# A two-layer GELU block on one core: the first loads dealt out over three queues

## The chip, the cores and the metric

The kernel runs on one core of one Trainium2 chip. The metric is the device time of one execution in microseconds (us); lower is better. Of the kernel before there are seven runs without a profile, and one profiled execution from which all rows and durations below are taken.

## The reference

The input x has 2048 rows (tokens) of 448 features, all tensors are bfloat16, and two dense layers with a GELU between them are applied to each row:

```python
def _gelu(x):
    return jax.nn.gelu(x, approximate=True)

B, S, D, F = 1, 2048, 448, 1792

def reference(x, w1, b1, w2, b2):
    h = jnp.einsum("bsd,df->bsf", x, w1) + b1
    h = _gelu(h)
    return jnp.einsum("bsf,fd->bsd", h, w2) + b2
```

## The kernel before

**Staging.** The 2048 rows are handled in four chunks of 512 (`c` from 0 to 3). For each chunk layer 1 computes, for 14 blocks of 128 hidden features (`ft`), the transposed hidden tile `g[:, ft, chunk]`, with ScalarE applying bias and GELU from PSUM; layer 2 then uses those tiles as stationary operands and makes four tiles of 128 rows by 448 outputs, to which VectorE adds b2 before SyncE stores them. Everything is written out by hand as one list of operations per engine; a small helper (`Program`) gives each engine its list in the order in which the operations were recorded and puts semaphore waits ahead of those that need them. The order of a queue is therefore the order of the calls in the source.

**Contraction of 448.** It is cut into three slabs of 128 (`w1_sb`, `k` = 0, 1, 2) and a rest of 64 (`w1r`). Every matmul uses 64 rows of the array, and two of them, one on each half of the rows, run side by side (a "pair"). The rest of 64 lies in partitions 64 to 127 of `w1r` and is copied by VectorE to partitions 0 to 63 for half of the feature blocks (line 380, event `w1rU`).

**Loads.** All weights come over SyncE's queue, in this order: the first x chunk, the first piece of w1 (feature blocks 0 to 3, 384 KB, called w1(0) below), the first piece of its rest (blocks 0 to 3, 64 KB, w1r(0)), w1(1) (blocks 4 to 7, 384 KB), w1r(1) (blocks 4 to 13, 160 KB), w1(2) (blocks 8 to 13, 576 KB), w2 in two parts, b2, and then the other three x chunks, which the DMA transposes on the way. ScalarE's queue carries one load, the 3.5 KB of b1 as 14 rows, and it waits for VectorE to clear the tile `b1n`. Behind it on ScalarE is a one-column GELU into `junk` (line 175), which brings in the activation table.

**The first chunk.** It isn't transposed by the DMA. It lands in `xn` as 128 partitions by four row tiles `t`, each partition holding four consecutive rows of x. TensorE transposes each tile in three steps of 128 columns (`turn`, line 337, 12 transposes) into PSUM, VectorE (t = 0, 2) and ScalarE (t = 1, 3) copy the result into `xT` (line 344). The last 64 columns of the four tiles are first gathered by VectorE into `xr` (line 351), transposed two tiles at a time (line 358) and copied out four times (line 367). TensorE needs the identity matrix for this, made by GpSimd.

**Around it.** Ahead of the transposes TensorE multiplies ones with ones into an unused PSUM bank (`warm`, line 190): seven matmuls of 512 columns and one of 256. VectorE, when it is through with the copies of the first chunk, turns b1 into one column per feature block (`turn_b1`, four 32x32-block transposes on line 179 and a cast on line 181), and then makes the two `w1rU` copies.

**Layer 1 of the first chunk.** `Layer1.a` is the three slabs of a pair of feature blocks, `Layer1.b` the same on the other half of the rows plus the rest of 64, after which ScalarE takes the two tiles. The order is `L[0].a` and `L[1].a` on the first 256 rows, the same on the second 256, `L[0].b`, `L[2].a`, `L[1].b`, `L[3].a`, `L[2].b`, and so on. `L[0]` and `L[1]` need w1(0) and w1r(0), `L[2]` and `L[3]` need w1(1) and w1r(1), `L[4]` to `L[6]` need w1(2). All these matmuls are recorded by one helper, `mm`, and so stand on line 215, as those of layer 2 do.

Of the kernel before, what the change touches and what calls it, by code (L numbers as in the profile page):

```python
# [73 lines left out]
def bass_standalone__dense_activation_gelu__prompt_kernel(  # L74
# [8 lines left out]
    B, S, D = x.shape  # L83
    F = w1.shape[1]
    P = 128
    H = P // 2
    SC = 512
    HC = SC // 2
    assert B == 1 and S % SC == 0 and F == 14 * P and D == 3 * P + H
    x2, out2 = x[0], out[0]  # L90
    NSC, NST, STC, NFT = S // SC, S // P, SC // P, F // P
    NPAIR = NFT // 2
    KT = 3
    D3 = KT * P
    DH = D // 2
    NWARM = 7

    with ExitStack() as es:
        sb = lambda name, shape, dt: es.enter_context(nc.sbuf_tensor(name, shape, dt))
        xn = sb("xn", [P, STC, D], BF16)  # L100
        xr = sb("xr", [P, STC // 2, P], BF16)
        ident = sb("ident", [P, P], BF16)
# [5 lines left out]
        b1n = sb("b1n", [32, P], BF16)  # L108
# [8 lines left out]
        pr = Program(nc, es)  # L117
# [7 lines left out]
        def w1_of(ft):  # L125
            return max(i for i, c in enumerate(W1CUTS) if c <= ft)

        def load_w1(i):
            c0, c1 = W1CUTS[i] * P, W1CUTS[i + 1] * P
            pr.dma("sync", lambda e: e.dma_start(  # L130
                w1_sb[:, :, c0:c1], w1[0:D3, c0:c1].rearrange("(k p) f -> p k f", p=P)), ("w1", i))

        RCUTS = (0, 4, 14)
# [1 line left out]
        def load_w1r(i):  # L135
            cs = slice(RCUTS[i] * P, RCUTS[i + 1] * P)
            pr.dma("sync", lambda e: e.dma_start(w1r[H:P, cs], w1[D3:D, cs]), ("w1r", i))
# [12 lines left out]

        x0v = x2[0:SC, :].rearrange("(p t) d -> p t d", t=STC)
        o0v = out2[0:SC, :].rearrange("(p t) d -> p t d", t=STC)
        pr.dma("sync", lambda e: e.dma_start(xn[:, :, :], x0v), "x")  # L153
        load_w1(0)
        load_w1r(0)
        load_w1(1)
        load_w1r(1)
        load_w1(2)
        load_w2(0, 7)
        load_w2(7, 14)  # L160
        pr.dma("sync", lambda e: e.dma_start(b2_bc[:, :], b2.partition_broadcast(P)), "b2")
        for c in range(1, NSC):
            for slot in range(KT + 1):
# [6 lines left out]
            base=0, pattern=[[-1, P]], channel_multiplier=1), after=["ident0"], event="ident")  # L170
        pr.op("gpsimd", lambda e: e.memset(b2_z[:, :], 0.0), event="b2z0")
        pr.op("vector", lambda e: e.memset(b1n[:, :], 0.0), event="b1z")  # L172
        pr.dma("scalar", lambda e: e.dma_start(b1n[0:NFT, :], b1.rearrange("(c p) -> c p", p=P)), "b1n",
               after=["b1z"])
        pr.op("scalar", lambda e: e.activation(junk[:, :], one, ACT.Gelu_apprx_tanh))  # L175

        def turn_b1():
            for q in range(4):
                pr.op("vector", lambda e, q=q: e.transpose(  # L179
                    b1t[32 * q:32 * q + 32, :], b1n[:, 32 * q:32 * q + 32]), after=["b1n"], event=("b1t", q))  # L180
            pr.op("vector", lambda e: e.tensor_copy(b1_f[:, :], b1t[:, 0:NFT]),
                  after=[("b1t", q) for q in range(4)], event="b1")
# [5 lines left out]
        def warm(n, cols=SC):  # L188
            for _ in range(n):
                pr.op("tensor", lambda e: e.matmul(unit[2][:, 1, 0:cols], lhsT=ones_w, rhs=ones_m[:, 0:cols],  # L190
                                                   start=True, stop=True))
# [140 lines left out]
        def stage(t):  # L332
            return unit[3 - t // 2][:, t % 2, 0:2 * P].bitcast(BF16)

        def turn(t):
            for k in range(KT):
                pr.op("tensor", lambda e, k=k: e.transpose(  # L337
                    stage(t)[:, k * P:(k + 1) * P], xn[:, t, k * P:(k + 1) * P], ident[:, :]),
                    after=["ident", "x"], event=("xt", t) if k == KT - 1 else None)

        def evac(engine, t):
            o = xT[:, 0:KT, t * P:(t + 1) * P]
            i = stage(t)[:, 0:D3].rearrange("p (k s) -> p k s", k=KT)
            pr.op(engine, lambda e: e.copy(o, i) if engine == "scalar" else e.tensor_copy(o, i),  # L344
                  after=[("xt", t)], event=("xT0", t))
            busy[(3 - t // 2, t % 2)] = ("xT0", t)

        def turn_all():


            pr.op("vector", lambda e: e.tensor_copy(
                xr[:, :, :].rearrange("p q (two h) -> p q two h", two=2),
                xn[:, :, D3:D].rearrange("p (q two) h -> p q two h", two=2)), after=["x"], event="xr_in")
            for t in range(STC):
                turn(t)
                evac(("vector", "scalar")[t % 2], t)
            for q in range(STC // 2):
                pr.op("tensor", lambda e, q=q: e.transpose(
                    stage(0)[:, q * P:(q + 1) * P], xr[:, q, :], ident[:, :]),
                    after=["xr_in", ("xT0", 0)], event=("xr", q))  # L360
            halves = (slice(0, H), slice(H, P))
            for src, engine in enumerate(("vector", "scalar")):
                i = stage(0)[halves[src], 0:2 * P].rearrange("p (q s) -> p q s", q=2)
                for dst in (src, 1 - src):
                    o = xT[halves[dst], KT, 0:SC].rearrange("p (q two s) -> p q two s", q=2, two=2)[:, :, src, :]
                    pr.op(engine, lambda e, o=o, i=i, engine=engine:
                          e.copy(o, i) if engine == "scalar" else e.tensor_copy(o, i),  # L367
                          after=[("xr", 0), ("xr", 1)], event=("xR0", dst, src))
            busy[(3, 0)] = ("xR0", 1, 0)
            busy[(3, 2)] = ("xR0", 0, 1)  # L370

        warm(NWARM)
        warm(1, HC)
        turn_all()
        turn_b1()

        for i in (0, 1):
# [3 lines left out]
                  after=[("w1r", i)], event=("w1rU", i))  # L381
# [12 lines left out]
        for c in range(NSC):  # L394
# [7 lines left out]
            else:  # L402

                pr.op("vector", lambda e: e.tensor_copy(b2_z[H:H + 1, :], b2_bc[H:H + 1, :]),  # L404
                      after=["b2", "b2z0"], event="b2z")
# [3 lines left out]
            p = Layer2(c, (0, 1))  # L409
            if c + 1 < NSC:  # L410
                q = Layer2(c, (2, 3))
# [5 lines left out]
            else:  # L417
                q, r = Layer2(c, (2,)), Layer2(c, (3,), True)
# [37 lines left out]
```

## Time and profile before

| what | value |
|---|---|
| median of 7 runs | 94.23 us (94.01 to 94.62) |
| the profiled execution's own time | 94.71 us |
| its span, first to last instruction | 93.4 us |
| TensorE matmul busy | 90.0 us (96%), 931 instructions |
| ScalarE busy | 38.5 us (41%) |
| VectorE busy | 13.4 us (14%) |
| first matmul of layer 1 | at 6.12 us |
| loads from HBM, written back | 3.79 MB, 1.84 MB |

The profile's page gives busy time of each engine, the chain of work that ended last and the costliest groups of instructions. Times in the views are us from the start of the span. PE is TensorE's matmuls, PEld its weight loads, DVE VectorE, ACT ScalarE, POOL GpSimd, SP SyncE; a q behind a name is the engine's queue of DMA issues. Names of tiles are shown without numbers, so that `w_sb` is either weight of the two layers and `u` any of the four PSUM units. The 1.3 us between span and time (94.71 less 93.4) lie outside of what the profile shows.

### The profile page before, as it was taken

What the parts mean: (1) busy time and instruction counts of PE and PEld (TensorE: products, weight loads), DVE (VectorE), ACT (ScalarE), POOL (GpSimd) and SP (SyncE); (2) the same over time, 40 slices, a digit from 0 to 9 for tenths busy, and PEclk for the clock granted to TensorE, in tenths of its full rate; (3) what the DMA queues carried; (4) which work ended last, traced back from release to release, by engine and by line L of the source; (5) the groups of instructions that cost most, each with busy time, mean ns of one, the idle gap of its engine ahead of it and who ended that gap; (6) DMA issues with size and microseconds to landing.
All of it is one profiled execution on the core that took longest, in us unless ns stands there. A gap on an engine that the chain in (4) does not pass through costs nothing.

```text
span 93.4 us, 2058 instructions
## 1 busy us (share of the span) xinstructions
PE 90.0 (96%) x931; PEld 46.6 (50%) x931; DVE 13.4 (14%) x33; ACT 38.5 (41%) x63; POOL 1.1 (1%) x7
## 2 busy tenths in 40 slices
PE   6989999999999999999999999999999999999990
PEld 2465444555544444455554444455554444475890
DVE  0173101010334000000234000000234000000421
ACT  3373787900002787900002888900001878910001
POOL 4000000000000000000000000000000000000000
PEclk9999999999999999999999999999999999999999
DMA  1999999754937100000032000000022000000022
GB/s 55 316 265 273 378 357 97 142 113 91 107 74 193 46 0 0 7 0 0 0 105 98 0 0 4 0 7 0 0 98 98 0 7 0 0 0 7 21 78 98
DMA packets 12340, 7.32 MB, mean 78 GB/s; under 512 B 6956, under 2 KB 12140, under 8 KB 12332
## 3 DMA queue, kind: packets, MB, share of 16 engines
q1 hardware_dynamic: 12304, 7.20, 32.6%
q8 instruction: 7, 0.11, 0.5%
q14 instruction: 1, 0.01, 0.0%
q10 hardware_dynamic: 28, 0.00, 0.0%
HBM read 3.79 MB, written 1.84 MB: 60 GB/s over the span
## 4 chain that ended last, share of the span: by engine, by line
PE 91%; DMA 5%; SPq 0%; DVE 0%; issue 0%
PE u L215 91%; DMA w_sb<-in_w_dram 5%; SPq L153 0%; DVE out_sb L324 0%
## 5 line engine op out<-in xcount | busy, mean ns | idle before, releaser
L267 ACT ACTIVATE g<-u,b_f 128x512 bf16<-128x512 f32 x56 | 35.0, 685 | 40.2 <-PE u L215 40.2
L215 PE MATMUL u<-w_sb,g 64*128 64x448 bf16 (+1 forms) x504 | 43.2, 328 | 0.0
L215 PE MATMUL u<-xT,w_sb 64*128 64x512 bf16 (+1 forms) x348 | 40.9, 369 | 0.4 <-DMA w_sb<-in_w_dram 0.4
L215 PEld LDWEIGHTS u<-w_sb,g 64*128 64x128 bf16 x504 | 24.5, 94 | 18.4
L215 PEld LDWEIGHTS u<-xT,w_sb 64*128 64x128 bf16 x348 | 16.8, 94 | 19.6 <-DMA w_sb<-in_w_dram 0.9
L310 DVE TENSOR_TENSOR out_sb<-u,b_bc 128x448 bf16<-128x448 f32 x14 | 8.1, 619 | 60.0 <-PE u L215 60.0
L215 PE MATMUL u<-xT,w1r 64*128 64x512 bf16 x56 | 10.6, 376 | 0.0
L215 PEld LDWEIGHTS u<-xT,w1r 64*128 64x128 bf16 x56 | 2.8, 94 | 3.3
L327 ACT CAST out_sb<-u 128x224 bf16<-128x224 f32 x1 | 0.3, 345 | 9.2 <-PE u L215 9.2
L190 PE MATMUL u<-const-bfloat16-1.0 128*128 128x512 bf16 (+1 forms) x8 | 3.4, 598 | 0.8 <-PEq L441 0.8
L190 PEld LDWEIGHTS u<-const-bfloat16-1.0 128*128 128x128 bf16 x8 | 1.0, 136 | 2.4 <-issue 2.4
L175 ACT ACT_TABLE_LOAD x1 | 1.3, 1283 | 1.6 <-DVE b1n L172 1.6
L344 ACT COPY xT<-u 128x384 bf16<-128x384 bf16 x2 | 1.0, 478 | 2.0 <-PE u L337 2.0
L337 PEld LDWEIGHTS u<-ident,xn 128*128 128x128 bf16 x12 | 1.2, 144 | 0.6 <-issue 0.6
L337 PE MATMUL u<-ident,xn 128*128 128x128 bf16 x12 | 1.4, 310 | 0.0
L185 DVE COPY xT<-xT 64x512 bf16<-64x512 bf16 x3 | 0.9, 290 | 3.8 <-DMA xT<-in_x_dram 3.8
L404 DVE COPY b_z<-b_bc 1x448 bf16<-1x448 bf16 x1 | 0.3, 268 | 5.4 <-DMA b_bc<-in_b_dram 5.4
L318 DVE TENSOR_TENSOR out_sb<-u,b_bc 128x448 bf16<-128x448 f32 x1 | 0.6, 624 | 1.7 <-PE u L215 1.7
L179 DVE STREAM_TRANSPOSE b1t<-b1n 32x32 bf16<-32x32 bf16 x4 | 0.8, 202 | 0.1
L344 DVE COPY xT<-u 128x384 bf16<-128x384 bf16 x2 | 0.7, 358 | 0.7 <-PE u L337 0.7
L380 DVE COPY w1r<-w1r 64x256 bf16<-64x256 bf16 (+1 forms) x2 | 0.6, 288 | 1.5 <-DMA w1r<-in_w_dram 1.4
L367 ACT COPY xT<-u 64x256 bf16<-64x256 bf16 x2 | 0.7, 368 | 0.0
(17 smaller groups left out, 4.1 us busy)
## 6 DMA issues: line engine op xcount, KB each, us to landing
out_dram<-out_sb SPq DMA_DIRECT2D x16, 112.0 KB, 1.7
w_sb<-in_w_dram SPq DMA_DIRECT2D x2, 784.0 KB, 9.5
w_sb<-in_w_dram SPq DMA_DIRECT2D x2, 384.0 KB, 5.4
w_sb<-in_w_dram SPq DMA_DIRECT2D x1, 576.0 KB, 7.3
xn<-in_x_dram SPq DMA_DIRECT2D x1, 448.0 KB, 3.2
xT<-in_x_dram SPq DMA_TRANSPOSE x12, 4.5
w1r<-in_w_dram SPq DMA_DIRECT2D x1, 160.0 KB, 6.5
b_bc<-in_b_dram SPq DMA_DIRECT2D x1, 112.0 KB, 9.6
```

Of the source, the lines that this page charges most:

```text
L175: pr.op("scalar", lambda e: e.activation(junk[:, :], one, ACT.Gelu_apprx_tanh))
L179: pr.op("vector", lambda e, q=q: e.transpose(b1t[32 * q:32 * q + 32, :], b1n[:, 32 * q:32 * q + 32]), after=["b1n"], event=("b1t", q))
L185: pr.op("vector", lambda e: e.tensor_copy(xT[0:H, KT, s0:s1], xT[H:P, KT, s0:s1]), after=after, event=event)
L190: pr.op("tensor", lambda e: e.matmul(unit[2][:, 1, 0:cols], lhsT=ones_w, rhs=ones_m[:, 0:cols], start=True, stop=True))
L215: o = pr.op("tensor", lambda e: e.matmul(unit[u][:, lo, cols], lhsT=lhsT, rhs=rhs, start=start, stop=stop, skip_group_check=skip), after=a ...
L267: pr.op("scalar", lambda e, lo=lo, ft=ft: e.activation(g[:, ft, c * SC:(c + 1) * SC], unit[u][:, lo, :], ACT.Gelu_apprx_tanh, bias=b1_f[:, ...
L310: pr.op("vector", lambda e, lo=lo, j=j: e.tensor_tensor(out=out_sb[:, j, :], in0=unit[u][:, lo, 0:D], in1=b2_bc[:, :], op=ALU.add), after= ...
L318: pr.op("vector", lambda e: e.tensor_tensor(out=out_sb[:, j, :].rearrange("p (two h) -> p two h", two=2), in0=unit[u][:, :, 0:DH], in1=b2_ ...
L337: pr.op("tensor", lambda e, k=k: e.transpose(stage(t)[:, k * P:(k + 1) * P], xn[:, t, k * P:(k + 1) * P], ident[:, :]), after=["ident", "x ...
L344: pr.op(engine, lambda e: e.copy(o, i) if engine == "scalar" else e.tensor_copy(o, i), after=[("xt", t)], event=("xT0", t))
L367: e.copy(o, i) if engine == "scalar" else e.tensor_copy(o, i),
L380: pr.op("vector", lambda e, odd=odd: e.tensor_copy(odd(slice(0, H)), odd(slice(H, P))), after=[("w1r", i)], event=("w1rU", i))
```

## The change

The first x chunk is loaded as two halves (row tiles 0 and 1, row tiles 2 and 3), one from SyncE's queue and one from ScalarE's, with a semaphore each; each row tile's transposes wait for their own half, and the gathering copy into `xr` becomes two copies. w1(1) leaves SyncE's queue and is issued from ScalarE's, recorded behind the one-column GELU. b1's load moves from ScalarE's queue to GpSimd's, behind the three operations that GpSimd does at the start. The warm-up becomes six matmuls of 512 columns.

```diff
-    NWARM = 7
+    NWARM = 6
...
-        def load_w1(i):
+        def load_w1(i, engine="sync"):
             c0, c1 = W1CUTS[i] * P, W1CUTS[i + 1] * P
-            pr.dma("sync", lambda e: e.dma_start(
+            pr.dma(engine, lambda e: e.dma_start(
...
-        pr.dma("sync", lambda e: e.dma_start(xn[:, :, :], x0v), "x")
+        for h, engine in ((0, "sync"), (2, "scalar")):
+            pr.dma(engine, lambda e, h=h: e.dma_start(xn[:, h:h + 2, :], x0v[:, h:h + 2, :]), ("x", h))
         load_w1(0)
         load_w1r(0)
-        load_w1(1)
         load_w1r(1)
         load_w1(2)
...
-        pr.dma("scalar", lambda e: e.dma_start(b1n[0:NFT, :], b1.rearrange("(c p) -> c p", p=P)), "b1n",
+        pr.dma("gpsimd", lambda e: e.dma_start(b1n[0:NFT, :], b1.rearrange("(c p) -> c p", p=P)), "b1n",
                after=["b1z"])
         pr.op("scalar", lambda e: e.activation(junk[:, :], one, ACT.Gelu_apprx_tanh))
+        load_w1(1, "scalar")
...
-                    after=["ident", "x"], event=("xt", t) if k == KT - 1 else None)
+                    after=["ident", ("x", t // 2 * 2)], event=("xt", t) if k == KT - 1 else None)
...
-            pr.op("vector", lambda e: e.tensor_copy(
-                xr[:, :, :].rearrange("p q (two h) -> p q two h", two=2),
-                xn[:, :, D3:D].rearrange("p (q two) h -> p q two h", two=2)), after=["x"], event="xr_in")
             for t in range(STC):
+                if t % 2 == 0:
+                    pr.op("vector", lambda e, t=t: e.tensor_copy(
+                        xr[:, t // 2, :].rearrange("p (two h) -> p two h", two=2), xn[:, t:t + 2, D3:D]),
+                        after=[("x", t)], event=("xr_in", t // 2))
                 turn(t)
...
-                    after=["xr_in", ("xT0", 0)], event=("xr", q))
+                    after=[("xr_in", q), ("xT0", 0)], event=("xr", q))
...
         warm(NWARM)
-        warm(1, HC)
```

## The prediction

> **What bounds the kernel now.** I read the chain of waits first, in order of time.
>
> ```profile
> 1.19 4.89 DMA w_sb<-in_w_dram
> 6.08 0.05 issue
> 6.12 85.08 PE u L215 x909
> ```
>
> From 6.12 us TensorE is the chain without a break to the end, 85.08 us long. Ahead of it stands one load: w1(0), issued at 1.19, landed at 6.08. Nothing that the change touches lies behind 16.5 us, where layer 2 begins, so its worth is how much earlier or later layer 1 of the first chunk starts, and whether it then still runs through. Next the timeline of TensorE's matmuls and the other engines over the first microseconds (start, us, engine, line, operation).
>
> ```profile
> 0.77 3.36 PE L190 MATMUL u<-const-bfloat16-1.0 128*128 128x512 bf16 x8 [0.77 <-PEq L441]
> 3.96 0.23 DVE L351 COPY xr<-xn 128x256 bf16<-128x256 bf16 x1 [3.04 <-DMA xn<-in_x_dram]
> 4.07 1.44 PE L337 MATMUL u<-ident,xn 128*128 128x128 bf16 x12
> 5.30 0.42 PE L358 MATMUL u<-ident,xr 128*128 128x128 bf16 x2
> 6.12 2.13 PE L215 MATMUL u<-xT,w_sb 64*128 64x256 bf16 x30 [0.40 <-DMA w_sb<-in_w_dram]
> 8.29 0.98 PEld L215 LDWEIGHTS u<-xT,w_sb 64*128 64x128 bf16 x12 [0.21 <-DMA w_sb<-in_w_dram]
> 0.95 0.62 ACTq L173 DMA_DIRECT2D b1n<-in_b_dram  x1
> 1.60 1.28 ACT L175 ACT_TABLE_LOAD   x1 [1.60 <-DVE b1n L172]
> ```
>
> x lands just before 3.96, the transposes are over at 5.72, TensorE waits 0.40 us, for w1(0) and not for x. The weight load at 8.29 shows a second wait: `L[2].a` needs w1(1), which arrives with nothing to spare. The source line of w1's three loads gives their times from issue to landing, and the windows how full the DMA engines are meanwhile (columns: window, its length, PE, PEld, DVE, ACT, POOL busy, granted clock, DMA share, GB/s).
>
> ```profile
> DMA to landing us min/median/max: 4.9/6.0/7.3
> ...
> 1.50:3.20 1.70, 1.70 (x5) 0.59 (x4) 0.00 (x0) 1.49 (x2) 0.37 (x1) 1.00 0.76 264
> 3.20:4.70 1.50, 1.50 (x10) 0.81 (x9) 0.34 (x2) 0.00 (x0) 0.00 (x0) 1.00 0.96 282
> 4.70:6.10 1.40, 1.03 (x10) 0.76 (x8) 0.87 (x3) 1.00 (x3) 0.00 (x0) 1.00 0.97 297
> 6.10:8.30 2.20, 2.18 (x32) 1.58 (x34) 1.51 (x8) 0.69 (x2) 0.00 (x0) 1.00 1.05 231
> 8.30:11.00 2.70, 2.70 (x28) 1.27 (x28) 0.35 (x1) 2.25 (x4) 0.00 (x0) 1.00 1.07 353
> ```
>
> With the issues at 1.19, 2.25 and 3.41 (SP's queue) the three land at 6.08, 8.25 and 10.7. The engines' share is 0.96 and more from 3.2 us on: they are full, and the order of the bytes is what decides.
>
> **x in two halves, and the warm-up.** The 448 KB of x move in the windows up to 3.2 us; TensorE sees them complete at 3.95, so some 0.7 us pass between the last bytes and the wait's end. If the first half goes first, its 224 KB are through by about 2.5 (half of 1.75 to 3.2) and it lands near 3.2. Six warm-ups at 0.43 each (weight loads of line 190 at 2.01, 2.43, 2.86) end at 0.77 + 6 x 0.43 = 3.35, so the transposes begin at about 3.4 instead of 4.07. The second half lands where x lands now, 3.95; tiles 0 and 1 take 6 x 0.107 = 0.64, to 4.05, so tiles 2 and 3 do not wait. All 14 transposes end near 5.05 instead of 5.72. That is 0.65 us less on a branch which already waits 0.40 for w1(0): worth nothing alone. The `xr` gather becomes two copies of some 0.2 us; the second waits for the second half on VectorE, with the copy of tile 2 queued behind it, which needs the same half. Cover: the same wait for w1(0).
>
> **w1(0) against w1(1).** Bytes ahead of w1(0) stay the same, x's 448 KB, for both halves are issued with it or before. New is a rival on another queue. ScalarE issues the second half at about 0.73, taking 0.4 to 0.6 (rows of SP's first issue, 0.39, and of b1, 0.62), loads its table for 1.28 and runs the GELU for 0.20, so that w1(1) is issued near 2.8; x's first data came 1.0 after its issue, hence w1(1)'s at about 3.75. By then w1(0) has had 3.75 - 3.2 = 0.55 us at 282 GB/s, 155 thousand of its 393 thousand bytes (384 KB). Shared equally, the other 238 thousand take 1.69 instead of 0.84 us: w1(0) lands **0.84 later**. If ScalarE's queue issues without waiting for the table load, the two share from 3.2 on, and 393 thousand bytes take 2.79 instead of 1.39: **1.39 later**. The other end: taking turns may be coarse. The DMA view by window has b1's packets (queue q10) as evidence: issued at 0.95, none moved before 3 us, all of them between 3.0 and 3.5, as x's last ones left.
>
> ```profile
> q1 hardware_dynamic: 101, 0.14, 80.5%
> q10 hardware_dynamic: 28, 0.00, 4.7%
> ```
>
> If w1(1) stands behind w1(0) in that way, the cost is 0. Below nothing: if two queues fill the engines better, at the 353 GB/s of the last window instead of some 275, the 852 thousand bytes of x and w1(0) take 2.41 instead of 3.10 us, but some of that lies in the slow first microsecond; I take **0.5 earlier** as that end. Within -0.5 to +1.39 I take +0.65, nearer to the case worked out from ScalarE's own rows (+0.84) than to 0, because b1's row speaks for turns that are not fine.
>
> The Trainium skill, DMA: Bandwidth & Descriptors, section "Issuing engines are not separate DMA queues", holds that DMAs of all queues run on the same 16 engines and interleave, so that a second queue saves only the issuing time. It speaks against this change; by it alone the sum would be +0.84 to +1.39, and the rows of full engines agree with its first half, while b1's row does not show an even interleaving.
>
> **w1(1) and those behind it.** It is needed 2.18 us after the start (8.30 less 6.12), at 8.95 if the start is 6.77. From 3.75 at half of 231 to 282 GB/s its 393 thousand bytes take 2.8 to 3.4, to 6.6 to 7.2, and 1.4 to 2 more pass to the landing as for w1(0): 8.0 to 9.2. Cost 0 to 0.25 (no gain is possible, since at that start it is not the last to arrive); I take 0. SP moves w1r(1) and w1(2) up past it. w1(2) is needed 5.2 after the start (`L[4].a` at 11.33 now, 12.0 then), landed at 10.7, and the bytes ahead of it are the same: 0. The issues behind (w2, b2, transposes) move up by one issue, 0.58, and are not waited for before 15 us: 0.
>
> **b1 by GpSimd.** No DMA of GpSimd is in the trace. It can be issued at 1.87 (line 171's memset, 1.40 + 0.47). The nearest row is b1 on ScalarE's queue: 2.5 us from issue to its last packet, which gives 4.4. VectorE takes it up behind its `xT` copies, now at 6.47, then perhaps 5.9. Behind it on VectorE are the cast and the `w1rU` copies; their chain of 4 x 0.20 + 0.18 + 0.22, some 1.5 us with gaps, must be over at the first rest pair, 1.97 after the start (8.09 now, 8.74 then). So b1 may land as late as 7.2, 2.8 us more than the nearest row; cost 0. Without that cover it is one for one, and the upper bound is b2's 9.6 us landing, the longest of a small load here: 11.5, which would cost 4; I hold that far from the nearest row and leave it in the tail.
>
> **The sum.** 0 + 0.65 + 0 + 0. On the profiled execution's 94.71 us (span 93.4) this is 95.36; that execution lies 0.48 above the median, and on the median it is 94.23 + 0.65 = **94.9 us**. About 0.5% (0.47 us) is what a measurement here can tell from no change.
>
> **Rivals.**
> *Two queues fill the engines (faster).* w1(0) lands at about 5.6, x's branch is done at 5.05 plus the copies, and layer 1 starts 0.5 earlier: 93.7. For it: 264 to 297 GB/s now against 353 later, and the last engines' lag of 1.4 us behind the bytes. Against it: shares of 0.96 and more, and w1(1) then has to land 0.5 earlier also, at 7.8, or `L[2].a` takes the gain back. It decides once w1(0) lands before 5.65.
> *The load is as late as before (same).* Turns are so coarse that w1(1) waits for w1(0), the start stays near 6.1, and the earlier x is waste: 94.2. b1's packets speak for it.
> *The clock comes late (slower).* Warm-ups of 512 columns stand 0.43 apart, six pairs of 512 in layer 1 take 1.30 (8.30 to 9.60), 0.22 each: the rate doubles somewhere between 5.4 and 6.12, although the granted clock reads 1.00 throughout. Now TensorE idles 0.40 before layer 1; afterwards from 5.05 to 6.77, 1.7 us. If the doubling is put off, each us of layer 1 at the old rate costs 0.5, and at most the 4.95 us (0.77 to 5.72) that it takes now: up to 2.5, and with half of it on top of 0.65 96.1. The Trainium skill, TensorE: Matmul & The Clock Gate, section "Why this matters for your kernels", asks for 4 us of continuous work and allows gaps up to about 3 us; by it this term would be nothing, and no row here shows a gap of 1.7 us.
>
> **How the numbers follow.** Main case, w1(0) later by 0.2 to 1.4: 0.44, of which 0.08 stays within 0.47 us. Faster rival 0.26. Same rival 0.17. Late clock 0.13. Faster 0.26; same 0.17 + 0.08 = 0.25; slower 0.36 + 0.13 = 0.49. The range goes from 93.6, just below the faster rival, to 96.1; the main case alone spans 94.4 to 95.6.
>
> **What would show it.** Right: transposes from about 3.4; w1(0) landing at 6.5 to 7.1 and heading the chain; queue q10 moving w1(1) between 3.5 and 7; 256-column pairs of layer 1 standing 0.11 apart. Wrong: w1(0) landed by 5.65; the weight load of `L[2].a` or VectorE's b1 transposes with a wait of over 0.3 us; 256-column pairs in layer 1 standing 0.21 apart instead of 0.11.

## The result, and the profile after

The changed kernel takes 96.04 us at the median of 12 runs (94.99 to 98.85), against 94.52 (94.00 to 94.77) of the kernel before in 31: slower by 1.31% (ratio 1.0131, 95% interval 1.0106 to 1.0157). The profiled execution takes 96.14 us and spans 94.8. The ratio leaves out executions that lie over 1.5% above the fastest of the same kernel; since one cause found below costs about that much, the medians here are over all runs.

The sign and the range of the forecast (94.9 us, 93.6 to 96.1) hold, the range by 0.06 us: 96.04 lies outside the main case's 94.4 to 95.6, and the medians are 1.52 us apart where 0.65 was forecast. The way there is another one. The chain of waits of the kernel after, in order of time (start, us, what):

```profile
1.20 4.45 DMA w_sb<-in_w_dram
5.65 0.05 issue
5.70 86.96 PE u L216 x909
```

w1(0) landed at 5.65, 0.43 us *earlier* than in the profile before, and layer 1 started 0.42 earlier. But the same 909 matmuls on line 216 (215 before) now last 86.96 us instead of 85.08. The timeline of the first microseconds shows where (start, us, engine, line, operation; the last bracket is the idle time before it and its releaser):

```profile
0.78 2.72 PE L191 MATMUL u<-const-bfloat16-1.0 128*128 128x512 bf16 x6 [0.78 <-PEq L442]
1.18 1.28 ACT L175 ACT_TABLE_LOAD   x1 [1.18 <-PEq L442]
1.24 0.44 ACTq L130 DMA_DIRECT2D w_sb<-in_w_dram  x1
3.94 1.44 PE L338 MATMUL u<-ident,xn 128*128 128x128 bf16 x12 [0.43 <-DMA xn<-in_x_dram]
5.70 4.02 PE L216 MATMUL u<-xT,w_sb 64*128 64x256 bf16 x30
7.15 0.90 DVE L180 STREAM_TRANSPOSE b1t<-b1n 32x32 bf16<-32x32 bf16 x4 [0.86 <-DMA b1n<-in_b_dram]
9.09 0.15 PEld L216 LDWEIGHTS u<-xT,w1r 64*128 64x128 bf16 x2 [0.27 <-DVE w1r L381]
9.51 0.42 PE L216 MATMUL u<-xT,w1r 64*128 64x512 bf16 x2
9.77 1.46 PE L216 MATMUL u<-xT,w_sb 64*128 64x512 bf16 x12
```

Before, the first rest pair of layer 1 stood at 8.09, 1.97 after the start at 6.12:

```profile
8.09 0.38 PE L215 MATMUL u<-xT,w1r 64*128 64x512 bf16 x2
```

The first 30 matmuls take 4.02 us instead of 2.13, and the first rest pair comes 3.81 after the start instead of 1.97: 1.84 us later, for TensorE is still at its first, half rate. Twelve pairs of 256 columns at 0.213 and three of 512 at 0.427 make 3.84. The next row, 12 matmuls in 1.46, is again as before. So 1.84 less the earlier start of 0.42 is 1.42, and the spans differ by 1.4: this execution loses all of it to TensorE's rate doubling at about 9.5 us instead of before 6.12. Ahead of it is a pause: the warm-up ends at 3.50, the transposes begin at 3.94. The wait for b1 (0.86 on VectorE, then 0.27 for a weight load) is hidden: VectorE finished both `w1rU` copies (0.49 us from 8.39 on) while TensorE was still at half rate.

The third row also corrects the order of ScalarE's queue: w1(1) was issued at 1.24, beside the table load and not behind it. Two windows (columns as in the prediction) show the engines fuller than before, 374 GB/s against 282 and 327 against 297:

```profile
3.20:4.70 1.50, 1.07 (x9) 0.80 (x9) 0.45 (x2) 0.00 (x0) 0.00 (x0) 1.00 1.06 374
4.70:6.10 1.40, 1.29 (x14) 0.90 (x13) 0.94 (x5) 1.15 (x3) 0.00 (x0) 1.00 1.13 327
```

The second queue isn't shown to be the reason. The kernel before with only b1's load moved (below), whose x and weights all come over SyncE's queue, moved 352 GB/s in the first of these windows and started layer 1 at 5.67:

```profile
3.20:4.70 1.50, 1.50 (x10) 0.79 (x9) 0.32 (x2) 0.00 (x0) 0.00 (x0) 1.00 1.07 352
```

### The profile page after: what moved, and what is told of

The parts are those of the page before. It is cut to its first block, busy times and chain, and to the rows that moved or that the text cites. A ratio compares the mean times of both kernels' runs of the same rounds, so it can differ in the third digit from the quotient of the medians.

```text
span 94.8 us, 2056 instructions
## 1 busy us (share of the span) xinstructions
PE 91.3 (96%) x929; PEld 46.8 (49%) x929; DVE 13.4 (14%) x34; ACT 38.5 (41%) x63; POOL 1.7 (2%) x8
## 3 DMA queue, kind: packets, MB, share of 16 engines
HBM read 3.79 MB, written 1.84 MB: 59 GB/s over the span
## 4 chain that ended last, share of the span: by engine, by line
PE 92%; DMA 5%; SPq 0%; DVE 0%; issue 0%
PE u L216 92%; DMA w_sb<-in_w_dram 5%; SPq L154 0%; DVE out_sb L325 0%
## 5 line engine op out<-in xcount | busy, mean ns | idle before, releaser
L216 PE MATMUL u<-xT,w_sb 64*128 64x512 bf16 (+1 forms) x348 | 42.7, 383 | 0.1
L216 PEld LDWEIGHTS u<-xT,w_sb 64*128 64x128 bf16 x348 | 17.5, 98 | 20.3 <-issue 0.5
L191 PE MATMUL u<-const-bfloat16-1.0 128*128 128x512 bf16 x6 | 2.7, 626 | 0.8 <-PEq L442 0.8
```

The source lines that it names most:

```text
L216: o = pr.op("tensor", lambda e: e.matmul(unit[u][:, lo, cols], lhsT=lhsT, rhs=rhs, start=start, stop=stop, skip_group_check=skip), after=a ...
```

## The experiments

Theories: **A**, the clock (the shorter warm-up leaves a pause, and the rate doubles late); **B**, b1 by GpSimd lands late; **C**, w1(1) on ScalarE's queue costs, by delaying w1(0) as the prediction had it or otherwise; later **D**, the parts work on one another, and **E**, C's loss comes from what SyncE sends meanwhile.

| kernel | median of all runs (range) | ratio to before (95%) |
|---|---|---|
| changed | 96.04 (94.99 to 98.85) | 1.0131 (1.0106 to 1.0157) |
| changed, old warm-up | 95.49 (94.96 to 96.74) | 1.0093 (1.0055 to 1.0132) |
| changed, b1 from ScalarE's queue | 95.99 (94.67 to 97.19) | 1.0101 (1.0059 to 1.0144) |
| both: only the loads of x and w1(1) changed | 94.88 (94.51 to 95.42) | 1.0045 (1.0024 to 1.0067) |
| before, short warm-up | 94.44 (93.93 to 96.44) | 0.9978 (0.9956 to 0.9999) |
| before, w1(1) on ScalarE's queue | 95.30 (94.42 to 96.59) | 1.0059 (1.0021 to 1.0097) |
| before, b1 by GpSimd | 94.46 (94.05 to 95.01) | 1.0012 (0.9991 to 1.0033) |
| before, x in halves | 94.41 (93.97 to 94.82) | 0.9993 (0.9968 to 1.0018) |
| before, w1(1) on ScalarE's queue and short warm-up | 95.81 (95.03 to 98.12) | 1.0136 (1.0092 to 1.0181) |
| only the loads, w1(1) after x's first half | 99.08 (97.40 to 99.95) | 1.0337 (1.0305 to 1.0370) |
| only the loads, SyncE held | 94.51 (94.02 to 94.78) | 1.0003 (0.9986 to 1.0020) |
| changed, SyncE held | 94.90 (94.68 to 98.36) | 1.0034 (1.0013 to 1.0055) |
| only the loads, SyncE held, short warm-up | 94.44 (94.05 to 96.22) | 1.0005 (0.9981 to 1.0029) |

Of 128 runs of the kernel before, taken beside these, one lies above 95.2 us, at 96.67.

**The changed kernel with the old warm-up.**

```diff
-    NWARM = 6
+    NWARM = 7
...
         warm(NWARM)
+        warm(1, HC)
```

> The changed kernel with the old warm-up (seven matmuls of 512 columns and one of 256). Theory A, the clock: the changed kernel loses because TensorE pauses 0.43 us between its shorter warm-up and the first transposes, so that the rate doubles only at about 9.5 us and layer 1's first 1.84 us are paid twice. Here the pause is gone: pairs of 256 columns stand 0.11 us apart from the first one. If A were all, layer 1 starts at 5.7 to 5.9 and the time is 94.0 to 94.3. Theory B, b1 by GpSimd: b1 lands only at 7.1, VectorE then makes the copy for the rest of 64 (w1rU) at 8.4 to 8.6, while TensorE at the full rate would want it at about 7.6: a stall near 1 us, which the slow clock hid before. A and B together: 94.9 to 95.2, with a wait for VectorE in front of the first rest pair. If neither holds and the loads are to blame, about 96 as in the changed kernel.

0.55 us less than the changed kernel at the median, and more than the 94.9 to 95.2 of A and B together. The runs of the two kernels overlap so far that the difference of the medians isn't clear of the spread. The profile says more: it has no pause, and the rate doubled before layer 1:

```profile
6.44 2.13 PE L216 MATMUL u<-xT,w_sb 64*128 64x256 bf16 x30 [1.38 <-DMA w_sb<-in_w_dram]
7.49 0.90 DVE L180 STREAM_TRANSPOSE b1t<-b1n 32x32 bf16<-32x32 bf16 x4 [1.72 <-DMA b1n<-in_b_dram]
9.01 0.09 PEld L216 LDWEIGHTS u<-xT,w1r 64*128 64x128 bf16 x1 [0.72 <-DVE w1r L382]
```

30 matmuls take 2.13 again, as A has it. B shows too, as a wait of 0.72 that the slow clock had hidden. And here w1(0) is what TensorE waits for, until 6.40: it came 0.7 later than in the profiled execution of the changed kernel, out of the same queues. Where w1(0) lands is not settled by the source. The 1.38 us for which TensorE stood idle there did not bring the half rate back.

**The changed kernel with b1 from ScalarE's queue.**

```diff
-        pr.dma("gpsimd", lambda e: e.dma_start(b1n[0:NFT, :], ...
+        pr.dma("scalar", lambda e: e.dma_start(b1n[0:NFT, :], ...
```

> The changed kernel with b1 loaded from ScalarE's queue again, behind the half of x and ahead of the table load; the short warm-up stays. Theory A alone or A with B: the clock still comes late, the missing copy was hidden by it, so 95.8 to 96.2, no wait of VectorE for b1, pairs of 256 columns 0.21 apart. Theory B alone: 94.5 to 95.0.

As A expects: the median is the changed kernel's within 0.05, and the profile has the late doubling.

```profile
5.68 3.81 PE L216 MATMUL u<-xT,w_sb 64*128 64x256 bf16 x30
```

**Both of these edits: only the loads of x and w1(1) are changed.**

> The changed kernel with the old warm-up and with b1 from ScalarE's queue: what is left of the change is x in two halves and w1(1) on ScalarE's queue. Theories A and B together: layer 1 starts at 5.7 to 5.9, runs through, 94.1 to 94.4 against 94.5 of before, since w1(0) landed 0.43 us earlier in the changed kernel. The theory of the prediction, that w1(1) on its own queue holds w1(0) up: 94.9 or more.

94.88 is slower than A and B together allow (94.1 to 94.4) and just short of what the prediction's theory asked. The start was early, at 5.32; the loss comes 3 us later (rows as above):

```profile
5.32 2.13 PE L216 MATMUL u<-xT,w_sb 64*128 64x256 bf16 x30
7.49 0.09 PEld L216 LDWEIGHTS u<-xT,w1r 64*128 64x128 bf16 x1 [0.31 <-DVE w1r L382]
8.47 1.47 PE L216 MATMUL u<-xT,w_sb 64*128 64x512 bf16 x12 [0.59 <-DMA w_sb<-in_w_dram]
```

w1(0) wins and w1(1) loses: issued at 1.94, it landed at 8.42, and `L[2].a` waits 0.59 for it. In the changed kernel itself w1(1) was in time. There b1 doesn't stand ahead of it on ScalarE's queue, it was issued at 1.24 and landed at 6.61 (at 7.24 with the old warm-up). The rows of w1(1) with KB and us from issue to landing, of the changed kernel and of this one:

```profile
w_sb<-in_w_dram ACTq DMA_DIRECT2D x1, 384.0 KB, 5.4
w_sb<-in_w_dram ACTq DMA_DIRECT2D x1, 384.0 KB, 6.5
```

So the stall of 0.59 was seen only with b1 on ScalarE's queue. The medians split the loss into 0.36 for the loads (94.52 to 94.88), 0.61 for b1 (to 95.49) and 0.55 for the warm-up (to 96.04). In the other order the warm-up costs 1.11 and b1 0.05, so some 0.56 of the loss can be put down to either of the two, and the split is no list of stalls in the changed kernel.

**The kernel before with the short warm-up alone.**

> The kernel before with the short warm-up alone (six matmuls of 512 columns). Theory A: x lands at 3.95, the warm-up ends near 3.5, a pause of 0.4 to 0.5 us as in the changed kernel, the rate doubles late; layer 1 starts at 6.1 at half rate: 95.9 to 96.6. Theory B or the loads: 94.5, the same as before.

A as stated fails here: 94.44, no slower than before. But the two slowest of its 12 runs are 95.37 and 96.44, and the one at 95.37 is the profiled one, with a pause of 0.70 and, for a part of the matmuls, the half rate (3.15 us for 30):

```profile
4.19 1.44 PE L337 MATMUL u<-ident,xn 128*128 128x128 bf16 x12 [0.70 <-DMA xn<-in_x_dram]
5.78 3.15 PE L215 MATMUL u<-xT,w_sb 64*128 64x256 bf16 x30
```

So, if the pause is the reason, it makes the late doubling possible and not certain.

**The parts, one by one, on the kernel before.** w1(1) alone on ScalarE's queue, b1 alone by GpSimd, x alone in halves, and w1(1) together with the short warm-up:

> The kernel before with w1(1) alone moved to ScalarE's queue, behind b1 and the one-column GELU; x in one piece, old warm-up. In the runs so far ScalarE's queue issued w1(1) right after the load ahead of it, without waiting for the table load. Theory C, the loads: w1(1) then moves beside x and w1(0) from about 2.6 us on, x or w1(0) lands 0.3 to 0.8 later or w1(1) itself is what TensorE waits for: 94.9 to 95.4. If two queues only fill the engines better: 94.0 to 94.4.

> The kernel before with b1's load alone moved to GpSimd. Theory B: b1 lands 5.3 to 5.6 us after its issue at 1.83, at 7.1 to 7.4, VectorE ends the copy for the rest of 64 at 8.6 to 8.9 instead of 7.93, TensorE wants it at 8.0: a wait of 0.5 to 0.8 and 95.0 to 95.3. Theories A or C alone: 94.5, the same as before.

> The kernel before with x alone in two halves on the two queues; w1(1) stays on SyncE's queue, b1 on ScalarE's, old warm-up. All theories: the order of the weights is as before, w1(0) lands at 5.7 to 6.1, the time is 94.2 to 94.6, the same as before. If the split of x itself is what spreads the landings: 94.9 or more.

> As the run with w1(1) alone on ScalarE's queue, with the short warm-up on top. The short warm-up alone cost nothing on the kernel before (ratio 0.9978) but 1.1 us at the median with x and w1(1) on two queues. Theory D: the short warm-up only hurts where the second queue makes TensorE pause a second time or longer before layer 1, so that the doubling slips: 95.8 to 97 here, with pairs of 256 columns 0.21 apart. If the two parts simply add: the time of w1(1) alone within 0.2 us.

x in halves does nothing, as expected. b1 by GpSimd alone does nothing either, which was a miss: its transposes on VectorE began at 6.48 without a wait, so b1 was there in time. With only SyncE's queue beside it, it landed 3.8 us after its issue; in the changed kernel and in the one with the old warm-up, with two full queues beside it, 5.3 and 5.6. w1(1) alone costs, but its median (95.30) has a range of 2.2 us, against 0.8 of the kernel with x in halves, and four of its 12 runs lie at 96.2 to 96.6, with the old warm-up. Its profile is of one of the better runs (94.63): w1(0) early, w1r(0) and w1(1) late, at 7.6 and 8.2. The last kernel's profile (98.12 us) is that of a poor run; no poor run of w1(1) alone was profiled. First the timeline of TensorE's matmuls, then two windows:

```profile
8.33 0.64 PE L215 MATMUL u<-xT,w1r 64*128 64x512 bf16 x2 [0.89 <-DMA w1r<-in_w_dram]
10.02 1.74 PE L215 MATMUL u<-xT,w_sb 64*128 64x512 bf16 x12 [1.05 <-DMA w_sb<-in_w_dram]
```

```profile
8.30:10.00 1.70, 0.64 (x2) 0.19 (x2) 0.58 (x2) 1.25 (x2) 0.00 (x0) 1.00 1.07 316
11.10:14.40 3.30, 3.30 (x18) 1.24 (x16) 0.00 (x0) 1.27 (x2) 0.00 (x0) 0.50 1.57 323
```

First w1r(0), then w1(1) is waited for, and after these two stalls the granted clock reads 0.50 from 11.1 to 14.4: the late loads cost a second time, by the clock. D's stated picture (256-column pairs 0.21 apart) is not what this execution shows, its early part ran at the full rate; that stalls for late loads were followed by the slow clock it does show. By the numbers, 1.36% against 0.59% for w1(1) alone; the intervals just overlap and only six runs stand behind it, so that the short warm-up adds to the cost of w1(1) is not shown by the times.

**Is it w1(0) that suffers, or w1(1)? w1(1) issued later, and SyncE held back.** Both start from the kernel with only the loads of x and w1(1) changed.

```diff
-        load_w1(1, "scalar")
+        load_w1(1, "scalar", [("x", 0)])        # waits for x's first half
```

> The run with x in halves and w1(1) on ScalarE's queue (old warm-up, b1 on ScalarE's queue), with w1(1)'s issue made to wait until the first half of x has landed, at about 3.8 us. The theory of the prediction: w1(1) started too early and took the engines from w1(0); a later start frees w1(0): 94.0 to 94.4. Theory E: the loss comes from what SyncE issues behind w1(0) (w1r(1), w1(2)), which shares the engines with w1(1) and w1r(0) and so makes these two, which TensorE needs at once, land late; a later start of w1(1) makes it worse: TensorE waits 1 us or more for w1(1), 95.4 to 96.5.

```diff
-        load_w1r(1)
+        load_w1r(1, [("w1", 0)])                # SyncE goes on after w1(0)
```

> The same run without that wait, but SyncE issues w1r(1), and all behind it, only after w1(0) has landed (about 5.3 us). Theory E: w1(1) and w1r(0) then have the engines nearly alone after w1(0), w1(1) lands near 7 instead of 8.4 and layer 1 runs through from about 5.4 on: 93.6 to 94.1, faster than before. The theory of the prediction: w1(0) is slowed by w1(1) as before, 94.7 to 95.0, no change against the run without the hold.

Issued at 3.96, after SyncE had queued w1(2) and the first part of w2, w1(1) took 7.3 us; TensorE waits 3.46 us for it (timeline), and the windows show the clock at 0.50 behind that:

```profile
11.33 1.89 PE L216 MATMUL u<-xT,w_sb 64*128 64x512 bf16 x8 [3.46 <-DMA w_sb<-in_w_dram]
```

```profile
7.90:11.30 3.40, 0.00 (x0) 0.00 (x0) 0.00 (x0) 1.20 (x2) 0.00 (x0) 0.92 1.09 373
11.30:14.20 2.90, 2.87 (x14) 1.05 (x16) 0.27 (x1) 0.00 (x0) 0.00 (x0) 0.50 1.31 265
```

The prediction's theory would have had this kernel faster; it is 3.4% slower, and at 99.08 us slower than E's 95.4 to 96.5 too. With SyncE held, w1(1) landed 5.1 us after its issue at 1.94, at 7.0, TensorE ran through, and the loss is gone (1.0003; 12 runs within 0.8 us). Its chain of waits:

```profile
5.85 0.04 issue
5.90 85.08 PE u L216 x909
```

So E holds for these kernels: with SyncE's later loads held back, w1(1) landed 1.4 us earlier than without the hold. The gain that E promised on top (93.6 to 94.1) did not come: w1(0) landed at 5.85 and TensorE still waits 0.33 for it.

**The hold in the changed kernel, and the short warm-up with the hold.**

> The changed kernel as it is (short warm-up, b1 by GpSimd), with SyncE's w1r(1) and all behind it held until w1(0) has landed. Theories D and E together: with the loads on time the short warm-up and b1 by GpSimd cost little, as each alone on the kernel before: 93.8 to 94.6. If the short warm-up is a cost of its own (the clock, whatever the loads do): 95 or more, with pairs of 256 columns 0.21 apart in the profile.

> The run with the hold on SyncE's queue (x in halves, w1(1) on ScalarE's queue, b1 on ScalarE's queue, w1r(1) and all behind it after w1(0)), with the short warm-up in place of the old one: with the loads on time this leaves the warm-up alone. Theory A: the doubling of TensorE's rate is then a matter of chance, part of the executions as without the short warm-up (94.0 to 94.8) and part 1.3 to 2 us longer, so that the median over all runs is 95 or more. If the warm-up does not matter: all runs within 94.0 to 94.9.

Both fall into two groups. The changed kernel with the hold has six runs at 94.68 to 94.90 and five at 96.28 to 98.36; with b1 back on ScalarE's queue, nine at 94.05 to 94.60 and three at 96.19 to 96.22; with the old warm-up as well, none of 12 above 94.78. So the short warm-up leaves most runs as they were and makes some 1.5 to 1.9 us longer, two of them 2.1 and 3.6, mostly the size of the late doubling in the profile after. No expectation fits as it stands: the two groups are A's, but A had a median of 95 or more in the last kernel, and D and E had 93.8 to 94.6 in the other. The lower groups differ by 0.4. Part of that may be b1: in the profiled execution at 94.81 a weight load waits for VectorE, which waited for b1:

```profile
6.79 0.90 DVE L180 STREAM_TRANSPOSE b1t<-b1n 32x32 bf16<-32x32 bf16 x4 [0.80 <-DMA b1n<-in_b_dram]
8.30 0.09 PEld L216 LDWEIGHTS u<-xT,w1r 64*128 64x128 bf16 x1 [0.55 <-DVE w1r L381]
```

In the last kernel's profile, with b1 in time, the same copy is waited for 0.47, layer 1 having started 0.42 earlier; so b1's own share can't be read from these two.

For the clock itself the 14 profiles can be counted, by the spacing of TensorE's matmuls. Eight have no pause between the warm-up and the transposes; their rate doubled between 3.7 and 6.4 us, in six before layer 1 and in two (b1 by GpSimd; x in halves) within its first two pairs. Six have a pause of 0.4 to 0.7 us, all with the short warm-up. Three of these doubled at 4.3 to 5.3 us, and three well inside layer 1, at 8.0 (the kernel before with the short warm-up), 9.1 (b1 from ScalarE's queue) and 9.5 (the changed kernel). Of the kernels whose loads came in time, 10 of 35 runs with the short warm-up lie above 95.3 us, and 1 of 164 with the old one. What decides among the six wasn't found. No execution of the upper groups was profiled, so that they are late doublings is inferred from their size.

## Why the prediction was right, and where it was not

**x in halves, no gain alone**: right (0.9993). The first half landed at about 3.8 (3.1 us after its issue at 0.75), not at 3.2, and the second at about 3.95 (3.2 after 0.74): both halves came almost together. The six warm-ups were put to an end at 3.35 for a landing near 3.2; they ended at 3.50 and left a pause of 0.43 that the prediction did not have.

**w1(0) later by 0.65**: wrong, and this is the term that carried the forecast. It landed at 5.65 in the changed kernel. w1(1)'s issue was put at 2.8, behind the table load; it was at 1.24. The prediction had a sum for that case too, and it gave 1.39 later. So the step that failed is the equal sharing at an unchanged rate. From 3.20 to 4.70 us SyncE's queue (q1) moved 0.36 MB and ScalarE's (q10) 0.21, at 374 GB/s together:

```profile
q1 hardware_dynamic: 357, 0.36, 67.1%
q10 hardware_dynamic: 201, 0.21, 39.2%
```

Nor is it shown that the second queue made w1(0) earlier. Over all 14 profiles it landed at 5.26 to 6.08 where SyncE carries all weights and at 4.99 to 6.39 where w1(1) is on ScalarE's queue, so the 6.08 that the sum started from was the late end of a spread. The rival of fuller engines had the start right, 0.42 earlier (it said 0.5), but its mechanism is not shown: 352 GB/s were reached with all weights on one queue.

**w1(1), cost 0 to 0.25, taken as 0**: right for the profiled changed kernel, where it landed at 6.61, well before the expected 8.0 to 9.2. Behind b1 on ScalarE's queue the place was right and the size wrong: 0.59 of waiting with only the loads changed, 1.05 in the worst execution of w1(1) with the short warm-up, 3.46 when issued later. The sum looked at bytes *ahead* of it; what counted was what SyncE had put on the engines beside it, as the run with SyncE held shows. **w1r(0) had no term at all**: TensorE waited 0.89 for it in the poor execution, where it landed at 8.28, 3.2 us after w1(0).

**b1**: landed 5.3 us after its issue at 1.83, at about 7.15, against a limit set at 7.2 and a guess of 4.4. The guess was too early by 2.7. The limit was worked out for a start of layer 1 at 6.77; with the start at 5.70 and the full rate, the same working gives about 6.1 (5.70 + 1.97 - 1.5, an estimate), and b1 missed that. It cost nothing in the profiled execution only because the slow clock covered it. With the clock on time the medians with and without b1 on GpSimd lie 0.4 to 0.6 apart, though the start of layer 1 differed as well.

**The late clock** was given 0.13 as a rival; it is what the profiled execution shows, 1.84 against a stated bound of 2.5, and what the changed kernel's upper runs are most likely made of. The prediction saw the pause in the wrong place, between the transposes and layer 1 (there it was 0.11); it was at the warm-up's end. The Trainium skill, TensorE: Matmul & The Clock Gate, section "Why this matters for your kernels", allows gaps to about 3 us between bursts of matmuls. The runs bear this out in one place and not in another: the idle time of 1.38 us with the old warm-up did not bring the half rate back, but two stalls of 0.89 and 1.05 us, 0.6 us apart, were followed by a granted clock of 0.50. The pause of 0.43 is no case of this rule; it stood behind 2.7 us of work, less than the 4 us without a break that the same section asks for first. Its Part 1 says that the activity window runs freely, so that the moment of doubling varies between executions; the two groups of runs and the doublings between 3.7 and 9.5 us agree with that, and nothing here shows where a window begins.

**The sum**: 0.65 was forecast at 94.23, 1.52 measured between the medians (0.36 loads, 0.61 b1, 0.55 warm-up, in that order). Slower was right, by a delay of w1(0) that the changed kernel's profile doesn't have. By its own signs the prediction was wrong: w1(0) had landed by 5.65, VectorE waited 0.86 for b1, and pairs of 256 columns stood 0.21 apart. That the time fell into the range, by 0.06 us, was luck in the main case; the upper end was there for the late clock, which is what came.

## What to carry to other kernels

When a load is moved to a second queue, list what the first queue will send beside it and who waits for each of those loads, not only for the load ahead: the last-needed piece of a full pipe simply becomes another. Before a second queue is blamed or praised, hold the first one back behind a landed load; one wait took the whole loss of 0.45% of the kernel with only the loads changed away. A warm-up is sized to the latest landing it has to bridge: a saving of 0.64 us of idle work bought nothing in most runs and cost 1.5 us or more in some, so look at all runs and not only at the median. And a landing read from one profile is one draw: w1(0)'s differed by up to 0.8 us between four kernels with all weights on one queue, more than the 0.65 that was to be forecast.

## What the runs showed of the hardware that was not expected

- A load on ScalarE's queue recorded behind an activation was issued while the table load ran (1.24 against 1.18 to 2.46).
- In the window from 3.20 to 4.70 us the engines moved 282 GB/s in the kernel before, 374 in the changed one, and 352 with all weights on one queue (b1 by GpSimd). The Trainium skill, DMA: Bandwidth & Descriptors, section "Issuing engines are not separate DMA queues", lets a second queue save only issuing time; these rows do not contradict it.
- Landings under two full queues vary between kernels with the same first loads: w1(0) at 5.65 and 6.39. w1(1) on ScalarE's queue landed 5.4 to 8.3 us after its issue, and 5.1 to 5.4 with SyncE held.
- b1's 3.5 KB, issued by GpSimd, landed 3.8 us after its issue beside one full queue and 5.3 and 5.6 beside two.
- The granted clock fell to 0.50 within 1.1 us after two stalls of 0.89 and 1.05 us, and in another kernel during a single stall of 3.46 us; both times it stayed so for about 3.4 us.
